# Linear attention with a gated feed-forward: loads held until a transposition has landed

## The chip, the cores and the metric

The kernel runs on one core of a Trainium2 chip. The metric is device time in microseconds (us), the median of several executions. A core has five engines with instruction streams of their own: TensorE (PE in the profile), VectorE (DVE), ScalarE (ACT), GpSimd (POOL) and SyncE (SP). They meet at semaphores. SP and POOL issue most of the DMA transfers, each on a queue of its own, and all queues share the core's 16 DMA engines. An engine executes its instructions in order, so an instruction that waits holds up everything behind it on the same engine.

## The reference

There are 8 batches, 8 heads, 576 positions and 64 dimensions per head. The attention is linear, with phi(x) = elu(x) + 1; then a gated feed-forward network:

```python
def phi(x):
    return np.where(x > 0, x, np.exp(x) - 1.0) + 1.0
q_p, k_p = (phi(q), phi(k))
kv = np.einsum('bhsd,bhse->bhde', k_p, v)
z = np.sum(k_p, axis=2)
num = np.einsum('bhsd,bhde->bhse', q_p, kv)
den = np.einsum('bhsd,bhd->bhs', q_p, z)[..., None] + 1e-06
x = (num / den)                    # to 4608 tokens x 512
a = x @ w1                         # 512 x 1024
b = x @ w2                         # 512 x 1024
h = a * b @ w3                     # 1024 x 1024
out = h @ w_out                    # 1024 x 512
```

## The kernel before

At the start w3 and w_out are multiplied into one 1024 x 512 matrix, so that the feed-forward of a chunk is two products with w1 and w2, an elementwise product, and one more matrix product. A chunk is 512 tokens of one batch; each batch also has a tail of 64 positions, and the tails of all eight batches make up a ninth chunk.

The whole kernel is a list of steps in one string, ORDER, which the last loop walks through. Nothing is rescheduled: the list gives the order of instructions on every engine. A step is a letter, a batch (or chunk) number and a part; a "+" moves it to another engine (for loads from SP to POOL, for copies from ACT to DVE). The letters that matter here:

- L, M, N: load half of a batch's k, q or v, 512 KB each (L95, on SP unless "+"). All three take their buffers from one pool of 13.
- R: load a batch's tail, part 0 for q and k (four transfers of 64 KB), part 1 for v (two) (L104). All R steps around the change are on POOL.
- x and X: the exponential of k and of q on ScalarE (L168). y and Y: max(x, 0) + 1 on DVE (L173). z and Z: the minimum of both, on DVE (L198; L193 for tails), which is phi in bf16. Part 2 is the tail. v: v converted into the tile that also carries a column of ones (L204, L210).
- T: the phi of q transposed by a DMA transposition, on SP (L249). It reads what Z.0, Z.1 and z.2 of that batch wrote.
- K: the kv product of a batch on TensorE (L225, L229) and its copy out of PSUM (L234).
- A: numerator and denominator of 128 positions (L280 on TensorE, reads T's tile), and then 1e-6, reciprocal and product on DVE (L284 to L286). K and A share one PSUM buffer, tagged "at".
- D: the result transposed for the feed-forward, by a DMA transposition on SP (L311). F: eight matmuls with w1 and w2 (L322), the copy of one result by ScalarE (a_sb, L327) and the product by DVE (L328); PSUM has room for two such F at a time. O: the last product (L479) and its copy into an output buffer (L481), two buffers in all. S: the store of an output buffer, 512 KB, on SP (L489).

The steps on SP around the change are, before: T2.0 L3.0 N3.1 L3.1 L4.0 N3.0 S0.1 T3.0 D2.0 S0.0 L4.1 N4.1 M4.0 M4.1 M6.1 D3.0 S1.0 M5.0 N4.0 M5.1 L5.0 T4.0 N5.1 S1.1 M6.0 L5.1 N5.0 N6.0 S2.1 N6.1 T5.0 D4.0 S2.0. On POOL: R4.1 R4.0 R6.0 R6.1 R7.0 R7.1. On PE: K3 O1.3 A3.0 O1.2 A3.2 F2.6 A3.3 F2.3 F2.1 and later F2.5 A3.4 O2.3 F3.7 A2.4; then K4, K5, O3.1, A5.2.

GATES is a second string: "X<Y" gives step X's load a dependency on the transfer of step Y, through `after`. In the kernel before it is empty.

Of the kernel before, what the change touches and what calls it, by code (L numbers as in the profile page):

```python
# [20 lines left out]
def kernel(  # L21
# [77 lines left out]
    def load_tail(b, part, alt):  # L99
        names = ("qk", "v")[part]  # L100
        t = raw[names + "r", b] = ldr.tile([P, len(names), RW], F32, tag="ldr" + names, name=names + "32r")
        for i, name in enumerate(names):
            for g in range(2):
                ins = (nc.gpsimd if alt else nc.sync).dma_start(  # L104
                    out=t[g * R:(g + 1) * R, i].rearrange("p (h d) -> p h d", d=D),
                    in_=src[name][b, g * 4:(g + 1) * 4, NJ * P:S, :].rearrange("h p d -> p h d"))
        return ins

# [137 lines left out]
    def qt_load(b, part):  # L246
        t, s = qt_tile(b), ph["qt", b]
        i = NB if part else 0
        nc.sync.dma_start(out=t[:, i:NB + 2], in_=s[:, i * P:(NB + 2) * P], transpose=True)  # L249

# [412 lines left out]
```

## Time and profile before

| | us |
|---|---|
| median of 3 runs (257.8 to 259.88) | 257.89 |
| the profiled execution's own time | 259.98 |
| its span, from the first to the last instruction | 256.4 |
| PE busy | 231.0 |
| DVE busy | 159.1 |
| ACT busy | 117.1 |
| POOL busy | 48.8 |

The granted clock of TensorE was 0.998 of full speed. All times in the prediction are from the start of the span. In a row of a timeline the first number is the start, the second the duration; then come engine, line, operation, what is written and read, and the count of instructions in the row; the bracket at the end holds the idle time of the engine before the row and what ended it. A row of SP is the time in which SP issued the transfer, not the transfer itself; the views by tile and of the DMA queues give the time from issue to landing.

### The profile page before, as it was taken

Reading aid. Unit: us, or ns where it says so; the run is one execution under the profiler, and the core shown is the slowest. Engines: PE = TensorE matmul, PEld = TensorE weight load, DVE = VectorE, ACT = ScalarE, POOL = GpSimd, SP = SyncE. Lnnn points to the kernel's source line nnn. Section 1 sums busy time; section 2 is a strip of 40 time slices with the busy share of each in tenths; the row PEclk is TensorE's granted clock in tenths of the full one; section 3 lists DMA queues with packets and bytes.
Section 4 is the critical chain, followed back from the end, with each engine's and each line's share of the span. In section 5 each row is a group of like instructions: output and inputs, shape, how many; then the busy total and the mean of one; then the engine's idle time right before and its main releaser. Section 6 shows DMA issues by size and latency. Waiting matters only on the chain.

```text
span 256.4 us, 3789 instructions
## 1 busy us (share of the span) xinstructions
PE 231.0 (90%) x1352; PEld 117.0 (46%) x1368; DVE 159.1 (62%) x350; ACT 117.1 (46%) x180; POOL 48.8 (19%) x84
## 2 busy tenths in 40 slices
PE   0087999999999859999999999999999999999994
PEld 0063665554454424445445445444544444444442
DVE  0548589777998525997887899987244642432300
ACT  2404677247756605756553383544423223233231
POOL 8634479364044300410000000000000000000000
PEclk9999999999999999999999999999999999999999
DMA  6999999999999999799999989736710343000144
GB/s 221 211 238 286 306 261 247 204 229 285 307 239 293 220 213 324 187 289 257 310 355 206 292 246 261 196 63 150 230 20 32 134 83 164 0 3 0 41 143 144
DMA packets 63890, 50.57 MB, mean 197 GB/s; under 512 B 33536, under 2 KB 58368, under 8 KB 63872
## 3 DMA queue, kind: packets, MB, share of 16 engines
q1 hardware_dynamic: 54576, 37.10, 57.2%
q0 software_dynamic: 9152, 13.11, 22.9%
q8 instruction: 10, 0.16, 0.3%
q10 hardware_dynamic: 144, 0.13, 0.1%
q14 instruction: 8, 0.07, 0.1%
HBM read 38.80 MB, written 9.44 MB: 188 GB/s over the span
## 4 chain that ended last, share of the span: by engine, by line
PE 68%; DMA 20%; DVE 4%; issue 3%; SPq 1%; POOL 1%; ACT 1%; DVEq 0%; ACTq 0%; POOLq 0%
PE b_ps L322 22%; PE a_ps L322 22%; PE o_ps L479 18%; DMA w3b<-in_moe_w_dram 9%; DMA out_dram<-o_sb 7%; DMA qk32r<-in_k_dram 3%; PE nd L280 3%; PE kvp L225 2%; SPq L311 1%; DVE y L173 1%; PE o_ps L504 1%; DVE vt L204 1%; ACT a_sb L327 1%; PE kvp L229 1%; DVE kj L198 1%
## 5 line engine op out<-in xcount | busy, mean ns | idle before, releaser
L322 PEld LDWEIGHTS <-w_sb 128*128 128x128 bf16 x576 | 55.1, 98 | 62.8 <-issue 1.6
L328 DVE TENSOR_TENSOR ab<-a_sb,b_ps 128x512 bf16<-128x512 f32 x72 | 49.0, 685 | 39.2 <-PE b_ps L322 28.5
L322 PE MATMUL a_ps<-xt,w_sb 128*128 128x512 bf16 x256 | 66.7, 379 | 0.7 <-ACT a_sb L327 0.6
L322 PE MATMUL b_ps<-xt,w_sb 128*128 128x512 bf16 x256 | 66.7, 379 | 0.2 <-ACT a_sb L327 0.2
L327 ACT COPY a_sb<-a_ps 128x512 f32<-128x512 f32 x72 | 41.8, 586 | 53.1 <-PE a_ps L322 48.7
L479 PE MATMUL o_ps<-wf_sb,ab 128*128 128x512 bf16 x267 | 62.7, 379 | 0.8 <-issue 0.2
L479 PEld LDWEIGHTS <-ab 128*128 128x128 bf16 x280 | 26.9, 98 | 29.9
L481 ACT COPY o_sb<-o_ps 128x512 f32<-128x512 f32 x29 | 16.8, 586 | 43.8 <-PE o_ps L479 33.4
L286 DVE TENSOR_TENSOR xn<-nd,r 128x512 bf16<-128x512 f32 x32 | 22.1, 691 | 1.1
L168 ACT ACTIVATE e<-q 128x1024 bf16<-128x1024 f32 x16 | 16.7, 1055 | 9.4 <-DMA q<-in_q_dram 9.4
L168 ACT ACTIVATE e<-k 128x1024 bf16<-128x1024 f32 x16 | 16.6, 1055 | 4.8 <-DMA k<-in_k_dram 4.8
L280 PE MATMUL nd<-kv,qt 128*128 128x130 bf16 (+1 forms) x160 | 15.8, 220 | 3.1 <-DMA qt<-qj 2.6
L280 PEld LDWEIGHTS <-qt 128*128 128x128 bf16 (+1 forms) x160 | 11.3, 99 | 14.4 <-DMA qt<-qj 3.1
L136 PE MATMUL w3p<-ident,w3b 128*128 128x128 bf16 x64 | 5.7, 242 | 13.2 <-DMA w3b<-in_moe_w_dram 13.2
L284 DVE TENSOR_SCALAR r<-nd 128x8 f32<-128x8 f32 (+1 forms) x40 | 6.4, 161 | 16.2 <-PE nd L280 15.8
L173 DVE TENSOR_SCALAR y<-q 128x1024 bf16<-128x1024 f32 x16 | 11.0, 693 | 7.9 <-DMA q<-in_q_dram 7.9
L143 PE MATMUL wf_ps<-wt_sb,w3t 128*128 128x512 bf16 x61 | 14.8, 379 | 0.8 <-DMA wt_sb<-in_moe_w_out_dram 0.7
L104 POOL DMA_DIRECT2D qk32r<-in_q_dram x14 | 9.0, 648 | 19.2 <-ACT a_sb L327 17.9
L225 PE MATMUL kvp<-vt,kj 128*128 128x130 bf16 x128 | 9.8, 219 | 2.8 <-DVE vt L204 2.0
L198 DVE TENSOR_TENSOR qj<-e,y 128x512 bf16<-128x512 bf16 x32 | 11.9, 416 | 0.4 <-ACT e L168 0.3
L204 ACT CAST vt<-v 128x1024 bf16<-128x1024 f32 x8 | 8.4, 1050 | 7.9 <-DMA v<-in_v_dram 7.9
L198 DVE TENSOR_TENSOR kj<-e,y 128x512 bf16<-128x512 bf16 x32 | 11.9, 418 | 0.2
(54 smaller groups left out, 176.4 us busy)
## 6 DMA issues: line engine op xcount, KB each, us to landing
out_dram<-o_sb SPq DMA_DIRECT2D x15, 512.0 KB, 3.5
q<-in_q_dram SPq DMA_DIRECT2D x13, 512.0 KB, 8.5
k<-in_k_dram SPq DMA_DIRECT2D x13, 512.0 KB, 6.5
v<-in_v_dram SPq DMA_DIRECT2D x12, 512.0 KB, 8.1
w3b<-in_moe_w_dram POOLq DMA_DIRECT2D x8, 256.0 KB, 12.1
...
```

What stands on the lines that cost most here:

```text
L143: nc.tensor.matmul(wfs[i], w3ts[i][:, kc, :], wo_sb[:, kc, :], start=(kc == 0), stop=(kc == FC - 1))
L168: nc.scalar.activation(out=e, in_=x, func=AF.Exp)
L173: (nc.gpsimd if alt else nc.vector).tensor_scalar(out=y, in0=x, scalar1=0.0, scalar2=1.0, op0=ALU.max, op1=ALU.add)
L198: nc.vector.tensor_tensor(out=p[0][:, 2 * g + c].rearrange("p j u d -> p u j d"), in0=e[:, c], in1=y[:, c], op=ALU.min)
L225: nc.tensor.matmul(kvp[:, i, g * W:(g + 1) * W], kj[:, hp, j].rearrange("p u d -> p (u d)"), vt[:, j, 2 * hp:2 * hp + 2, :].rearrange("p h ...
L280: nc.tensor.matmul(nd[rows, g, i * 2 * E1:(i + 1) * 2 * E1], w, kvs[b % 2][:, i, g].rearrange("p u e -> p (u e)"), start=True, stop=True)
L286: nc.vector.tensor_tensor(out=dst.rearrange("p (g h) e -> p g h e", g=2), in0=v4[:, :, :, 0:D], in1=r[rows].unsqueeze(3).to_broadcast([n, ...
L322: nc.tensor.matmul(ps, w[:, kc, f * P:(f + 1) * P], xt_of(c)[:, :, kc, :], start=(kc == 0), stop=(kc == KC - 1))
L327: nc.scalar.copy(out=a_sb, in_=a_ps)
L328: nc.vector.tensor_mul(out=abs_[c][:, f, :], in0=a_sb, in1=b_ps)
L479: nc.tensor.matmul(o_ps, ab[:, f, m * P:(m + 1) * P], wf_sb[:, f, :], start=(f == 0), stop=(f == FC - 1))
L481: copy_of(alt)(out=rows_of(c, m // 2)[:, m % 2], in_=o_ps)
```

## The change

Three things change. First, `load_tail` returns its first transfer instead of its last, `qt_load` returns its transposition, and T steps are remembered, so that GATES can name them: "R4.1<T3.0 R6.0<T4.0" makes POOL's load of batch 4's v tail wait for batch 3's transposition, and the load of batch 6's q and k tail for batch 4's. Second, on SP four loads move: L4.0 from ahead of N3.0 to behind S0.0, and M5.1, L5.0 and M6.1 to behind T4.0. Third, some phi steps move: v4.2, y4.2, x4.2 and z4.2 now stand together between F2.5 and Z4.0; Y5.1 stands behind K4; x6.2 and y6.2 stand behind L6.0. The set of steps is the same.

```diff
     def load_tail(b, part, alt):
         ...
+        first = None
         for i, name in enumerate(names):
             for g in range(2):
                 ins = (nc.gpsimd if alt else nc.sync).dma_start(
                     ...
-        return ins
+                first = first or ins
+        return first
     ...
     def qt_load(b, part):
         ...
-        nc.sync.dma_start(out=t[:, i:NB + 2], in_=s[:, i * P:(NB + 2) * P], transpose=True)
+        return nc.sync.dma_start(out=t[:, i:NB + 2], in_=s[:, i * P:(NB + 2) * P], transpose=True)
     ...
-    Y3.0 y5.2 z3.2 K2 F1.4 A2.2 X3.0 F1.3 L4.0 A2.3 x3.0 O0.1 Z3.0 A2.0 x3.1 N3.0 y3.0 O0.0 v3.1
-    S0.1 A2.1 y3.1 R5.1+ z3.0 z3.1 v3.0 v3.2 O1.1+ O1.0 T3.0 D2.0 S0.0 K3 R4.1+ R4.0+ O1.3 A3.0 O1.2
-    A3.2 L4.1 v4.2+ F2.6 A3.3 F2.3 N4.1 y4.1 F2.1 M4.0 x4.1 A3.1 x4.0 F2.0 M4.1 y4.2 M6.1 v5.2+ x4.2
-    F2.7 Y4.0 D3.0 F2.4 z4.1 X4.1 F2.2 Y4.1 v4.1 S1.0 F2.5 Z4.1 M5.0 N4.0 X4.0 Z4.0 A3.4 z4.2 y4.0
-    O2.3 F3.7 M5.1 Y5.0 v4.0 A2.4 F3.6 z4.0 L5.0 T4.0 R6.0+ x5.2 Y5.1 X5.0 F3.1 N5.1 Z5.0 S1.1 O2.2+
-    K4 F3.2 M6.0 x6.2 X5.1 A4.2 Z5.1 F3.4 z5.2 F3.5 y5.0 A4.1 F3.0 L5.1 F3.3 N5.0 y5.1 X6.1 y6.2
-    O2.1 A4.3 R6.1+ N6.0 S2.1 x5.1 N6.1 v5.0+ T5.0 O2.0 x5.0 v5.1+ A4.0 R7.0+ z5.1 D4.0 z5.0 X6.0
-    O3.3 y7.2 O3.2+ K5+ S2.0 L6.0 z6.2 O3.1 A5.2 L6.1 O3.0 A5.1 D1.1 Y6.1 Z6.1 F4.2 A5.0 Y6.0 F4.5
+    Y3.0 y5.2 z3.2 K2 F1.4 A2.2 X3.0 F1.3 A2.3 x3.0 O0.1 Z3.0 A2.0 x3.1 N3.0 y3.0 O0.0 v3.1 S0.1
+    A2.1 y3.1 R5.1+ z3.0 z3.1 v3.0 v3.2 O1.1+ O1.0 T3.0 D2.0 S0.0 L4.0 K3 R4.1+ R4.0+ O1.3 A3.0 O1.2
+    A3.2 L4.1 F2.6 A3.3 F2.3 N4.1 y4.1 F2.1 M4.0 x4.1 A3.1 x4.0 F2.0 M4.1 v5.2+ F2.7 Y4.0 D3.0 F2.4
+    z4.1 X4.1 F2.2 Y4.1 v4.1 S1.0 F2.5 Z4.1 v4.2+ M5.0 N4.0 X4.0 y4.2 x4.2 z4.2 Z4.0 A3.4 y4.0 O2.3
+    F3.7 Y5.0 v4.0 A2.4 F3.6 z4.0 T4.0 M5.1 L5.0 M6.1 R6.0+ x5.2 X5.0 F3.1 N5.1 Z5.0 S1.1 O2.2+ K4
+    Y5.1 F3.2 M6.0 X5.1 A4.2 Z5.1 F3.4 z5.2 F3.5 y5.0 A4.1 F3.0 L5.1 F3.3 N5.0 y5.1 X6.1 O2.1 A4.3
+    R6.1+ N6.0 S2.1 x5.1 N6.1 v5.0+ T5.0 O2.0 x5.0 v5.1+ A4.0 R7.0+ z5.1 D4.0 z5.0 X6.0 O3.3 y7.2
+    O3.2+ K5+ S2.0 L6.0 x6.2 y6.2 z6.2 O3.1 A5.2 L6.1 O3.0 A5.1 D1.1 Y6.1 Z6.1 F4.2 A5.0 Y6.0 F4.5
     ...
-    GATES = ""
+    GATES = "R4.1<T3.0 R6.0<T4.0"
     ...
         elif t == "T":
-            qt_load(b, i)
+            held[s] = qt_load(b, i)
```

## The prediction

> **What bounds the kernel now.** I read the page's head first, then the idle time in front of TensorE's instructions, then the chain that ended last, then the DMA queues behind it.
>
> ```profile
> span 256.4 us, 3789 instructions
> PE 231.0 (90%) x1352; PEld 117.0 (46%) x1368; DVE 159.1 (62%) x350; ACT 117.1 (46%) x180; POOL 48.8 (19%) x84
> ```
>
> TensorE is busy for 231.0 of 256.4 us, so the change can only win back idle time of PE, or add to it. In the timeline of PE from 59 us to the end only five rows carry idle time in front of them, and these three hold 4.01 us of it (the others have 0.23 and 0.16):
>
> ```profile
> 87.03 0.61 PE L225 MATMUL kvp<-vt,kj 128*128 128x130 bf16 x8 [0.80 <-ACT vt L204]
> ...
> 92.94 0.40 PE L280 MATMUL nd<-kv,qt 128*128 128x130 bf16 x4 [2.62 <-DMA qt<-qj]
> ...
> 99.79 1.02 PE L322 MATMUL a_ps<-xt,w_sb 128*128 128x512 bf16 x4 [0.59 <-ACT a_sb L327]
> ```
>
> In the written order these are K3 (batch 3's kv product), A3.0 (the first natural-layout product of batch 3, which reads the q that T3.0 transposes) and F2.1. After 111 us PE never waits again. The chain of work says what the third hangs on, and the timeline of SP says when things were issued:
>
> ```profile
> 75.05 12.37 DMA out_dram<-o_sb
> ...
> 88.21 3.46 SPq L311
> ...
> 91.77 6.31 DMA out_dram<-o_sb
> ...
> 99.25 0.50 ACT a_sb L327
> ```
>
> ```profile
> 73.30 1.00 SPq L95 DMA_DIRECT2D k<-in_k_dram  x2
> 74.39 0.57 SPq L95 DMA_DIRECT2D v<-in_v_dram  x1
> 75.05 1.98 SPq L489 DMA_DIRECT2D out_dram<-o_sb  x1
> 81.09 6.24 SPq L249 DMA_TRANSPOSE qt<-qj  x1
> 87.42 4.25 SPq L311 DMA_TRANSPOSE xt<-xn  x1
> ```
>
> The store S0.1 (75.05) lands at 87.42, and T3.0, ready at 81.09, holds SP until just then: a transposition's issue ends when what is ahead of it on the queue has drained. T3.0 itself lands at 92.9, where A3.0's wait ends. D2.0 and the store S0.0 queue behind it; S0.0 lands at 98.08 and frees the output buffer that ScalarE's copy for O1.3 needs, and behind that copy stand the a_sb copies that F2.1 waits for. So one backlog of transfers at 75 to 81 us costs all of the 4 us.
>
> The second limit is the DMA engines. In the table of windows, columns after DVE, ACT and POOL are the clock, the DMA share and GB/s:
>
> ```profile
> 124.00:134.00 10.00, 9.95 (x54) 4.79 (x54) 8.45 (x19) 5.01 (x8) 0.00 (x0) 1.00 1.10 372
> 88.00:92.00 4.00, 2.28 (x17) 1.11 (x15) 0.20 (x1) 1.07 (x3) 1.23 (x2) 1.00 1.56 101
> ```
>
> Saturated with 512 KB loads they move 372 GB/s, or 1.41 us for one load; with T3.0, D2.0 and tails together, 101.
>
> **The change, part by part.**
>
> *T3.0 freed of company.* Ahead of it or beside it went L4.0 (the second k of the row at 73.30, 512 KB) and, from POOL, these tails of batches 4 and 6:
>
> ```profile
> 74.25 1.23 POOL L104 DMA_DIRECT2D v32r<-in_v_dram  x2 [11.50 <-DVE vr L210]
> 75.47 1.29 POOL L104 DMA_DIRECT2D qk32r<-in_q_dram  x2
> 76.75 1.23 POOL L104 DMA_DIRECT2D qk32r<-in_k_dram  x2
> 77.97 1.23 POOL L104 DMA_DIRECT2D qk32r<-in_q_dram  x2
> 80.91 0.62 POOL L104 DMA_DIRECT2D qk32r<-in_k_dram  x1 [1.71 <-DMA v32r<-in_v_dram]
> ```
>
> Nine tails of 64 KB are 0.59 MB, 1.6 us at 372 GB/s; with L4.0 it is 3.0 us less. S0.1 then lands between 84.4 and (nothing saved) 87.4; I take 84.4. How long after the drain a transposition lands:
>
> ```profile
> 114.41 5.78 SPq L249 DMA_TRANSPOSE qt<-qj  x1
> ...
> DMA to landing us min/median/max: 7.8/7.8/7.8
> ```
>
> T4.0's issue ended at 120.19 and it landed at 114.41 + 7.8 = 122.2, 2.0 later; T3.0 needed 92.9 - 87.4 = 5.5, with tails beside it. So T3.0 lands between 86.4 and 89.9; I take 88, since no tail runs beside it now. The v load at 74.39, for which K3 waited 0.80, also comes sooner, so A3.0 is due at 92.94 - 2.62 - 0.80 = 89.5, after 88: both waits go. Every us by which T3.0 is later than 89.5 comes back in full. S0.0 landed 5.1 after T3.0; it now lands near 93.1, and up to 1.1 later because batch 4's six tails (0.39 MB, 1.1 us) enter right then. F2.1, due at 99.79 - 4.01 = 95.8, needs S0.0 plus the 1.7 us from 98.08 to 99.79, 94.8 to 95.9. Gain at F2.1: 4.0, between 1.5 (S0.0 2.5 late) and 4.0.
>
> *L4.0 behind S0.0.* It comes about 1.4 us ahead of L4.1, N4.1, M4.0 and M4.1 in the queue, but M6.1 leaves that group, so the five loads there are still five. I cost it at nothing: the exponentials of k wait behind F2.1's copy anyway.
>
> *POOL.* Its waiting instruction R4.1 has R4.0 behind it, R6.0 has R6.1, R7.0 and R7.1; POOL does nothing else after 42 us, so the waits hold up only tails. R4 is issued from 88 to 92 (six pieces at 0.65) and first read when DVE is past Z4.1, near 108. R7.0 is first read by y7.2:
>
> ```profile
> 137.01 0.42 DVE L173 TENSOR_SCALAR yr<-qk32r 128x512 bf16<-128x512 f32 x1
> ```
>
> Less the gain that is 134. R7.0 is the seventh to tenth of twelve pieces issued from T4.0's landing on (near 115, below), so issued by about 122: 12 us of cover for its landing. Without it DVE, and K5's copy behind y7.2, would be late by what is missing.
>
> *The phi steps of batch 4's tail.* Here DVE has new work at a tight place. In the timeline of DVE, the mul of F2.5, then Z4.1 and Z4.0 together, then the three operations of A3.4 (from 112.76), then z4.2:
>
> ```profile
> 110.70 0.69 DVE L328 TENSOR_TENSOR ab<-a_sb,b_ps 128x512 bf16<-128x512 f32 x1 [0.44 <-PE b_ps L322]
> 111.31 1.42 DVE L198 TENSOR_TENSOR qj<-e,y 128x512 bf16<-128x512 bf16 x4
> 112.76 0.17 DVE L284 TENSOR_SCALAR r<-nd 64x8 f32<-64x8 f32 x1
> ...
> 113.19 0.69 DVE L286 TENSOR_TENSOR xnr<-nd,r 64x512 bf16<-64x512 f32 x1
> 113.92 0.43 DVE L193 TENSOR_TENSOR qj<-er,yr 128x512 bf16<-128x512 bf16 x1
> ```
>
> ```profile
> 114.43 0.41 PE L280 MATMUL nd<-kv,qt 128*64 128x130 bf16 x4
> ```
>
> That PE row is A2.4. It writes the single PSUM buffer tagged "at" that A3.4's L286 reads until 113.88. The new order puts v4.2, y4.2 and z4.2 between F2.5's mul and A3.4's operations:
>
> ```profile
> 96.38 0.61 DVE L210 CAST vr<-v32r 64x256 bf16<-64x256 f32 x2
> ...
> 104.84 0.42 DVE L173 TENSOR_SCALAR yr<-qk32r 128x512 bf16<-128x512 f32 x1
> ```
>
> 0.61 + 0.42 + 0.43 = 1.46 us. F2.5's mul is released by PE (its own 0.44 of waiting says so), so nothing taken off DVE earlier helps. L286 ends at 113.88 + 1.46 = 115.34, 0.9 after A2.4 is due: a new wait of 0.9 us, between 0 (DVE elsewhere ahead) and 1.5. The gain from here is 3.1.
>
> *M5.1, L5.0 and M6.1 behind T4.0, twelve tails of 6 and 7 too.* T4.0 itself is now ready when DVE ends Z4.0, at 112.73 + 1.46 - 4.0 = 110.2, with little ahead. The price is at T5.0:
>
> ```profile
> 120.23 0.58 SPq L95 DMA_DIRECT2D v<-in_v_dram  x1
> ...
> 126.93 0.44 SPq L95 DMA_DIRECT2D v<-in_v_dram  x1
> 127.48 7.84 SPq L249 DMA_TRANSPOSE qt<-qj  x1
> ```
>
> From issue to landing, the load of 120.23 (N5.1) and the transposition of 127.48 (T5.0) took
>
> ```profile
> DMA to landing us min/median/max: 5.0/5.0/5.0
> ```
>
> ```profile
> DMA to landing us min/median/max: 11.7/11.7/11.7
> ```
>
> and A5.2, which reads T5.0's q, starts at
>
> ```profile
> 140.45 0.39 PE L280 MATMUL nd<-kv,qt 128*128 128x130 bf16 x4
> ```
>
> Today N5.1 lands at 125.2, T5.0 at 127.48 + 11.7 = 139.2, and A5.2 reads it at 140.45: only 1.3 us to spare. T5.0's issue ended at 135.3, when N6.1 had landed, seven transfers after N5.1 (1.44 us each); the landing followed 3.9 later. After the change A5.2 is due at 140.45 - 3.1 = 137.4. T4.0's issue, with nothing ahead, takes 2.7 us (T7.0's:)
>
> ```profile
> L249 SPq DMA_TRANSPOSE qt<-qj x1: 2671/2671/2671, 170.0 to 170.0; - x1
> ...
> DMA to landing us min/median/max: 4.5/4.5/4.5
> ```
>
> so M5.1 is issued at 113.0 and lands 5.0 later, at 118.0. Ten more transfers to N6.1 at 1.44 make 132.4; twelve tails, 0.79 MB, 2.1 us at 372 GB/s, make 134.5. T5.0 lands 2.0 (like T4.0) to 3.9 (like itself) later: 136.5 to 138.4. I take 138.4, its own row: a wait of 1.0 at A5.2, between 0 and the 5.7 of the third rival.
>
> The Trainium skill speaks against that price: Advanced Engine Details and Errata, section X-Bar Transpose (TRN2), says that transposing DMAs on this chip are as fast as regular ones. By it T5.0 would cost no more than a load's step, and the sum would be 1.0 better; the drain-to-landing figures above, 2.0 to 5.5 against 1.44, do not agree with it.
>
> *Sum.* 4.0 - 0.9 - 1.0 = 2.1 us. Against the profiled execution's 259.98 us (span 256.4, 3.6 around it) that is 257.9. The median of the runs shown is 2.1 below the profiled one; taking 2.1 off 257.89 gives **255.8**. The median run may lack some of the profiled stalls; that is in the second rival.
>
> **The rivals.**
>
> 1. *T5.0 hides.* If a transposition follows the drain by one load's step, 1.44, T5.0 lands at 135.9, A5.2 waits for nothing, the gain stays 3.1: 254.8; 253.9 if A2.4's wait also fails to appear. For it: T4.0's 2.0. Against: T5.0's 3.9. The rule of the Trainium skill quoted above is this case.
> 2. *It doesn't do what it says.* T3.0 and S0.0 land about as late as before, or the unprofiled runs had little to win there. If 1.5 of the 4.0 is won, and 0.9 lost at A2.4, the time is 257.3. For it: T3.0's 5.5 after the drain at 87.4 was long, and I know only that tails ran beside it; the profiled run is 2.1 above the median. Against: L4.0 and nine tails were plainly ahead of it or beside it.
> 3. *Slower: the tails of 6 and 7 choke the stretch before T5.0.* They enter in twelve pieces at 0.65 us on POOL, 7.8 us, among loads. If the engines then run as at 88 to 92, at 101 instead of 372 GB/s, 7.8 x (1 - 101/372) = 5.7 us are lost, T5.0 lands at 144.1, A5.2 starts 3.7 later than today: 261.5. It decides from 140.45: a T5.0 landing later than that makes the kernel slower. For it: that window. Against: T4.0 has landed when they start, and no transposition runs beside them until T5.0.
>
> **How the numbers follow.** Forecast 0.42 (own range 254.8 to 256.8: T5.0 between 137.4 and 139.4); rival 1 0.15; rival 2 0.25 (256.8 to 258); rival 3 0.18, half of it beyond 260.5. About 1% (2.6 us) is what a measurement can tell from no change. Faster by more than that (under 255.3): a third of the forecast and rival 1, 0.29. Slower by more (over 260.5): 0.13 with what I have not seen. The rest, 0.58, lies within 1%. The range 254.2 to 260.3 leaves out the best end of rival 1 and the worse half of rival 3.
>
> **What would show it.** T3.0 landing by 89.5 and no idle time before A3.0 shows the first step; S0.0 landing by 94 and none before F2.1, the second. A wait of some 0.9 us of nd for L286 near 111 us shows the squeeze on DVE. A wait of nd for qt near 137 us, and T5.0 landing within a us of 138.4, shows the fourth; waits of DVE for R7.0 at y7.2 would be a step that I have missed. The prediction is wrong if T3.0 lands late although alone, or if T5.0 lands after 140.45.

## The result, and the profile after

The changed kernel takes 257.29 us (median of 14 runs, 256.22 to 258.84), the kernel before 258.7 beside it (257.33 to 260.57). The ratio is 0.9955, with a 95% interval of 0.9933 to 0.9977: a gain of 0.45%, 1.2 us, where 2.1 were forecast. A ratio here is computed from the single executions, without those more than 1.5% above the fastest of their kernel, so it need not equal the ratio of the two medians, which are 1.41 us apart. The gain lies within the 1% that was called no change, inside the range, and is a little over half of what was worked out. The time itself, 257.29, is 1.5 above the forecast 255.8; 0.8 of that is the kernel before, which takes 258.7 over more runs and not 257.89. The span of the profiled execution went from 256.4 to 255.5. The page's head for the kernel after:

```profile
span 255.5 us, 3806 instructions
...
PE 233.0 (91%) x1368; PEld 117.4 (46%) x1368; DVE 159.4 (62%) x350; ACT 117.5 (46%) x180; POOL 48.2 (19%) x84
```

PE's busy time is 2.0 us longer with 1368 records in the trace against 1352, for the same matmuls; it says nothing on the work. So positions are compared, not busy times. These are the rows of PE's timeline from 59 us on that have idle time in front of them, in the kernel after; lines above 109 are two higher than before, L282 is L280 and L324 is L322:

```profile
70.93 1.02 PE L324 MATMUL b_ps<-xt,w_sb 128*128 128x512 bf16 x4 [0.32 <-ACT a_sb L329]
...
110.50 0.41 PE L282 MATMUL nd<-kv,qt 128*64 128x130 bf16 x4 [0.96 <-DVE xnr L288]
...
130.67 0.40 PE L282 MATMUL nd<-kv,qt 128*128 128x130 bf16 x4 [0.57 <-DVE xn L288]
...
138.51 0.40 PE L282 MATMUL nd<-kv,qt 128*128 128x130 bf16 x4 [1.01 <-DMA qt<-qj]
...
141.19 1.02 PE L324 MATMUL a_ps<-xt,w_sb 128*128 128x512 bf16 x4 [0.33 <-DMA xt<-xn]
...
152.03 1.02 PE L324 MATMUL b_ps<-xt,w_sb 128*128 128x512 bf16 x4 [0.28 <-ACT a_sb L329]
```

The first row stands ahead of what the change reaches. The others are A2.4, A4.0, A5.2, F4.2 and F4.1. The waits at K3, A3.0 and F2.1 are gone, as forecast; five smaller ones stand behind them. The two steps that waited longest before now start here, with no idle time ahead:

```profile
89.02 0.39 PE L282 MATMUL nd<-kv,qt 128*128 128x130 bf16 x4
...
94.88 1.03 PE L324 MATMUL a_ps<-xt,w_sb 128*128 128x512 bf16 x4
```

A3.0 at 89.02 and F2.1 at 94.88 are 3.92 and 4.91 us earlier than before. From there the lead is given back. The start of each step on PE, read from the two timelines, and how far the kernel after is ahead:

| step | before | after | ahead | lost since the row above, to |
|---|---|---|---|---|
| F2.5 | 108.70 | 103.74 | 4.96 | |
| A2.4 | 114.43 | 110.50 | 3.93 | 1.03, DVE's xnr (the squeeze) |
| A4.2 | 122.87 | 118.89 | 3.98 | |
| A4.0 | 133.91 | 130.67 | 3.25 | 0.73, DVE's xn |
| A5.2 | 140.45 | 138.51 | 1.94 | 1.31, T5.0's q |
| F4.2 | 142.63 | 141.19 | 1.44 | 0.50, D4.0's x |
| F4.4 | 153.89 | 152.89 | 1.01 | 0.43, ScalarE's a_sb |
| F5.7 | 157.80 | 156.93 | 0.87 | 0.14 |
| F7.0, the last F | 238.74 | 237.88 | 0.86 | 0.01 |

The column adds up: 4.96 - 1.03 - 0.73 - 1.31 - 0.50 - 0.43 - 0.14, and 0.04 of rounding and small shifts back, is 0.86; the spans differ by 0.88.

The transfers behind it, in SP's timeline of the kernel after. In order: T3.0, D2.0, S0.0, T4.0, N6.1, T5.0, D4.0.

```profile
81.20 2.67 SPq L251 DMA_TRANSPOSE qt<-qj  x1
84.07 3.16 SPq L313 DMA_TRANSPOSE xt<-xn  x1
87.32 0.53 SPq L491 DMA_DIRECT2D out_dram<-o_sb  x1
...
109.34 2.67 SPq L251 DMA_TRANSPOSE qt<-qj  x1
...
124.09 0.68 SPq L95 DMA_DIRECT2D v<-in_v_dram  x1
124.89 11.41 SPq L251 DMA_TRANSPOSE qt<-qj  x1
136.83 1.97 SPq L313 DMA_TRANSPOSE xt<-xn  x1
```

The views by line give the times from issue to landing; these are T3.0's, S0.0's, T4.0's, N6.1's, T5.0's and D4.0's:

```profile
DMA to landing us min/median/max: 6.4/6.4/6.4
...
DMA to landing us min/median/max: 4.4/4.4/4.4
...
DMA to landing us min/median/max: 4.6/4.6/4.6
...
DMA to landing us min/median/max: 12.2/12.2/12.2
...
DMA to landing us min/median/max: 13.6/13.6/13.6
...
DMA to landing us min/median/max: 4.3/4.3/4.3
```

T3.0 now lands at 87.6 (before 92.9), S0.0 at 91.7 (98.08), T4.0 at 113.9 (122.2). But T5.0 lands at 138.46 against 139.19, and D4.0 at 141.15 against 140.93: PE had five us of lead, and these two transfers are hardly earlier or not at all. That is the question for the experiments.

One row of DVE's timeline explains A4.0. It is y5.1, which stands ahead of A4.3's operations and waits for L5.1's k:

```profile
128.88 0.69 DVE L175 TENSOR_SCALAR y<-k 128x1024 bf16<-128x1024 f32 x1 [1.67 <-DMA k<-in_k_dram]
```

### The profile page after: what moved, and what is told of

The parts are those of the page before. It is cut to its first block, busy times and chain, and to the rows that moved or that the text cites. A ratio compares the mean times of both kernels' runs of the same rounds, so it can differ in the third digit from the quotient of the medians.

```text
span 255.5 us, 3806 instructions
## 1 busy us (share of the span) xinstructions
PE 233.0 (91%) x1368; PEld 117.4 (46%) x1368; DVE 159.4 (62%) x350; ACT 117.5 (46%) x180; POOL 48.2 (19%) x84
## 4 chain that ended last, share of the span: by engine, by line
PE 57%; DMA 28%; DVE 4%; issue 3%; POOL 3%; SPq 2%; ACT 1%; DVEq 0%; ACTq 0%; POOLq 0%
PE o_ps L481 18%; PE b_ps L324 17%; PE a_ps L324 17%; DMA k<-in_k_dram 7%; DMA v<-in_v_dram 5%; DMA out_dram<-o_sb 5%; DMA w_sb<-in_moe_w_dram 4%; DMA wt_sb<-in_moe_w_out_dram 3%; DMA qk32r<-in_q_dram 2%; PE nd L282 2%; PE kvp L227 2%; POOL w_sb L116 2%; SPq L313 1%; ACT a_sb L329 1%; PE o_ps L506 1%
## 5 line engine op out<-in xcount | busy, mean ns | idle before, releaser
L324 PEld LDWEIGHTS <-w_sb 128*128 128x128 bf16 x576 | 55.1, 98 | 63.0 <-issue 1.6
L324 PE MATMUL b_ps<-xt,w_sb 128*128 128x512 bf16 x256 | 66.7, 379 | 0.6 <-ACT a_sb L329 0.6
L324 PE MATMUL a_ps<-xt,w_sb 128*128 128x512 bf16 x256 | 66.7, 379 | 0.3 <-DMA xt<-xn 0.3
L481 PE MATMUL o_ps<-wf_sb,ab 128*128 128x512 bf16 x280 | 64.4, 379 | 0.0
L282 PE MATMUL nd<-kv,qt 128*128 128x130 bf16 (+1 forms) x160 | 15.8, 220 | 3.0 <-DMA qt<-qj 1.0
L282 PEld LDWEIGHTS <-qt 128*128 128x128 bf16 (+1 forms) x160 | 11.3, 99 | 14.5 <-DVE xn L288 3.0
L145 PE MATMUL wf_ps<-wt_sb,w3t 128*128 128x512 bf16 x64 | 16.0, 395 | 0.6 <-DMA wt_sb<-in_moe_w_out_dram 0.5
L175 DVE TENSOR_SCALAR y<-k 128x1024 bf16<-128x1024 f32 x16 | 11.0, 687 | 3.1 <-DMA k<-in_k_dram 3.0
L105 POOL DMA_DIRECT2D v32r<-in_v_dram x12 | 7.5, 630 | 26.4 <-DMA qt<-qj 25.3
```

Of the source, the lines that this page charges most:

```text
L105: ins = (nc.gpsimd if alt else nc.sync).dma_start(out=t[g * R:(g + 1) * R, i].rearrange("p (h d) -> p h d", d=D), in_=src[name][b, g * 4:( ...
L145: nc.tensor.matmul(wfs[i], w3ts[i][:, kc, :], wo_sb[:, kc, :], start=(kc == 0), stop=(kc == FC - 1))
L175: (nc.gpsimd if alt else nc.vector).tensor_scalar(out=y, in0=x, scalar1=0.0, scalar2=1.0, op0=ALU.max, op1=ALU.add)
L282: nc.tensor.matmul(nd[rows, g, i * 2 * E1:(i + 1) * 2 * E1], w, kvs[b % 2][:, i, g].rearrange("p u e -> p (u e)"), start=True, stop=True)
L324: nc.tensor.matmul(ps, w[:, kc, f * P:(f + 1) * P], xt_of(c)[:, :, kc, :], start=(kc == 0), stop=(kc == KC - 1))
L481: nc.tensor.matmul(o_ps, ab[:, f, m * P:(m + 1) * P], wf_sb[:, f, :], start=(f == 0), stop=(f == FC - 1))
```

## The experiments

The kernels were timed against the kernel before; a ratio is to that one. Diffs are of the tokens of ORDER and of GATES, against the changed kernel where nothing else is said. "Ahead" is PE's lead over the kernel before in the profiled executions, as in the table above.

### Each hold alone

Only the first hold: M5.1, L5.0 and M6.1 at their old places, the tails of 6 and 7 free to start when POOL gets to them.

```diff
-GATES = "R4.1<T3.0 R6.0<T4.0"
+GATES = "R4.1<T3.0"
-... F2.0 M4.1 v5.2+ ...  O2.3 F3.7 Y5.0 v4.0 A2.4 F3.6 z4.0 T4.0 M5.1 L5.0 M6.1 R6.0+ x5.2 X5.0 ...
+... F2.0 M4.1 M6.1 v5.2+ ...  O2.3 F3.7 M5.1 Y5.0 v4.0 A2.4 F3.6 z4.0 L5.0 T4.0 R6.0+ x5.2 Y5.1 X5.0 ...
     (and x6.2, y6.2 back to their old places)
```

> The first hold alone: R4 behind T3.0, L4.0 behind S0.0, batch 4's tail phi steps as in the change; M5.1, L5.0, M6.1 and the tails of 6 and 7 go where they went before, ahead of T4.0. Theory A (the second hold gives the gain back, because it pushes three loads and twelve tails, 2.2 + 4.2 us of transfer, into the stretch between T4.0 and T5.0): PE still stands 4.9 us earlier than before at F2.1, T4.0 lands near 117 and costs nothing, T5.0 lands near 134 and A5.2 waits for nothing; the gain kept is 3.5 to 4, about 255. Theory B (the engines are full from 81 to 139 us, so T5.0 lands near 138.5 in whatever order the same bytes go ahead of it): A5.2 waits 1 us as in the changed kernel, time within 0.5 of the changed kernel's 257.3.

259.92 us, ratio 1.0032 (0.9997 to 1.0066). F2.1 is 5.30 ahead, yet A4.2 is 1.04 behind. PE's idle rows:

```profile
107.19 0.82 PE L481 MATMUL o_ps<-wf_sb,ab 128*128 128x512 bf16 x3 [1.06 <-DVE ab L330]
...
112.63 0.41 PE L282 MATMUL nd<-kv,qt 128*64 128x130 bf16 x4 [1.42 <-DVE xnr L288]
...
123.91 0.40 PE L282 MATMUL nd<-kv,qt 128*128 128x130 bf16 x4 [2.73 <-DMA qt<-qj]
```

The last row is the reader of T4.0. The tails of 7, M5.1 and L5.0 are on their way beside T4.0, which is issued at 111.47 and lands at 123.86, where the kernel before had 122.22 and the changed one 113.91. So the lead won at T3.0 is lost one transposition later. Neither theory of the expectation saw this wait. That the second hold is what costs the changed kernel its gain falls with this: without it there is no gain.

Only the second hold: the kernel before, with M5.1, L5.0 and M6.1 behind T4.0, the gate R6.0<T4.0, and Y5.1, x6.2 and y6.2 moved with them. Against the kernel before (the three function changes that GATES needs are in):

```diff
-GATES = ""
+GATES = "R6.0<T4.0"
-... M4.1 y4.2 M6.1 v5.2+ ...  O2.3 F3.7 M5.1 Y5.0 ...  z4.0 L5.0 T4.0 R6.0+ x5.2 Y5.1 X5.0 ...
+... M4.1 y4.2 v5.2+ ...  O2.3 F3.7 Y5.0 ...  z4.0 T4.0 M5.1 L5.0 M6.1 R6.0+ x5.2 X5.0 ...
```

> The second hold alone: M5.1, L5.0, M6.1 behind T4.0 and the tails of 6 and 7 behind T4.0; L4.0, R4 and batch 4's tail phi steps as before. T3.0 has only R6's four tails less beside it (0.26 MB, 0.7 us), so A3.0 still waits about 2 us. Theory A: what is won there is small and T5.0 comes later than before (139.2) by the transfers pushed behind T4.0, less T4.0's own earlier landing: 140 to 143, a wait of 0 to 2 us at A5.2, time 0 to 2 us slower than before. Theory B: T5.0 again near 139, no wait at A5.2, 0.5 to 1 us faster than before.

259.38 us, ratio 1.0032 (1.0008 to 1.0056). T3.0 lands at 90.38, since the tails of 6 are out of its way by this gate too, and F2.1 is 2.98 ahead; but T5.0 lands at 140.56, 1.37 later than before, A5.2 waits 1.35 and is 0.16 behind; this is what theory A expected, not B. Each half alone is slower or no better, both together are faster. As these traces read, a hold pays only as long as the reader of the next transposition isn't reached by what was held.

### The gate on batch 4's tail

The changed kernel with only the gate of T4.0, so that R4 may run beside T3.0:

```diff
-GATES = "R4.1<T3.0 R6.0<T4.0"
+GATES = "R6.0<T4.0"
```

> The changed kernel with R4 free to load as early as before; only R6 and R7 are held. Six tails, 1.1 us at 372 GB/s or 1.9 at 0.31 each, are back ahead of T3.0. By the prediction T3.0 lands 1.1 to 2 us later, at 88.7 to 89.6, on the edge of A3.0's 89.0, so PE waits 0 to 0.6 there, and F2.1 has the rest of the gain. R4 is then out of the way of the loads after S0.0. Capacity theory: since T5.0 is still behind the same bytes it lands near 138.5 and the time is that of the changed kernel within 0.5.

258.25 us, ratio 0.9978 (0.9948 to 1.0009). T3.0 lands at 89.42 instead of 87.60, F2.1 is 4.41 ahead instead of 4.91, and the end 0.15 instead of 0.86. Not all of this is the gate's: in this profiled execution PE was already 0.45 behind at F1.5, ahead of what the change reaches, and T3.0 was issued 0.49 later. From issue to landing T3.0 takes 7.73 instead of 6.40, so six tails of 64 KB ahead of it or beside it cost it 1.3 us, 0.22 each, and PE read it without a wait all the same. The interval overlaps the changed kernel's: that the gate on batch 4's tail is worth anything is not shown.

### The phi steps of batch 4's tail

v4.2, y4.2 and z4.2 behind A3.4 take the squeeze on DVE away:

```diff
-F2.5 Z4.1 v4.2+ M5.0 N4.0 X4.0 y4.2 x4.2 z4.2 Z4.0 A3.4 y4.0
+F2.5 Z4.1 M5.0 N4.0 X4.0 x4.2 Z4.0 A3.4 v4.2+ y4.2 z4.2 y4.0
```

> The changed kernel, but v4.2, y4.2 and z4.2 behind A3.4's operations on DVE instead of ahead of them. Both theories: the wait of 0.96 us at A2.4 goes, and T4.0, which needs z4.2, is issued about 1 us later. A and B alike say that T5.0 then lands at the same time or up to 1 us later, so PE waits up to 1 us more at A5.2 and the time stays within 0.5 of the changed kernel's. If A2.4's wait were a loss of its own, the time would be 1.0 lower.

258.52 us, ratio 1.0012 (0.9981 to 1.0043). A2.4's wait is gone (5.03 ahead there), and nothing came of it. z4.2 is what T4.0 waits for, so T4.0 is issued 1.2 later and all loads behind it are too; L5.1 lands at 129.97, and y5.1 of DVE waits for it:

```profile
130.00 0.69 DVE L175 TENSOR_SCALAR y<-k 128x1024 bf16<-128x1024 f32 x1 [3.89 <-DMA k<-in_k_dram]
```

A4.0 then waits 2.80 us, and PE is 0.75 ahead at A5.2. About 1.4 us of the loss up to there has no wait in front of it: behind A4.0 the granted clock of TensorE falls to 0.53 from 131 to 134 us and 0.85 from 134 to 136, which is 1.7 us of its work. Eight of the twelve executions have a mean clock of 0.993 or less; the other four take 257.97 to 260.21, no less than the changed kernel. And T5.0 landed at 138.90, so that A5.2 could not have been more than 1.55 ahead. The 0.96 us at A2.4 were not won here: later waits take the same time back.

### Less in front of T5.0

The changed kernel once more, as a measure of how far one kernel differs from itself:

> The changed kernel once more, for comparison on the same chip: 0.993 to 0.998 of the kernel before. Slack theory (formed from the runs so far: the transfers from T5.0 on land when the bytes ahead of them are through, almost whatever the order, so what PE has won at a place cannot be more than the slack that the transfer read there had before, plus what it lands earlier): A5.2 stands 1.3 + (139.2 - T5.0's landing) us earlier than before, F4.2 1.7 + (140.9 - D4.0's landing).

257.39 us, ratio 0.9942 (0.992 to 0.9964), the same as the first time. In this profiled execution T5.0 landed at 137.59, A5.2 was 2.81 ahead and the end 1.78, so profiled executions of one kernel differ by 0.9. The loss behind A5.2 is the same in both: 1.08 and 1.03.

Two loads, M5.1 and L5.0, ahead of T4.0 again:

```diff
-... M5.0 N4.0 X4.0 ... F3.6 z4.0 T4.0 M5.1 L5.0 M6.1 R6.0+
+... M5.0 N4.0 M5.1 X4.0 ... F3.6 z4.0 L5.0 T4.0 M6.1 R6.0+
```

> The changed kernel with M5.1 and L5.0 ahead of T4.0 again; M6.1 and the tails of 6 and 7 stay behind it. In the changed kernel N4.0 has landed at 110.7 and the engines move 155 GB/s from 110 to 114, while T4.0 goes alone and SP holds nothing else. Capacity theory (T5.0 lands when the bytes ahead of it are through, so only an idle stretch of the engines that is filled brings it forward): the two loads land by 113.6, T4.0 by 115.6 to 116, ahead of A4.2 at 118.9, no wait there, and T5.0 lands 1.5 to 2.5 us earlier than 138.5, near 136.5; A5.2 waits for nothing; 1 to 2 us faster than the changed kernel. If T4.0's early landing is what makes the change faster, this is slower than the changed kernel.

256.95 us, ratio 0.9919 (0.9889 to 0.995). T5.0 was expected at 136.5, as the two loads were to fill an idle stretch of the DMA engines, and landed at 138.64, though two loads less stood between T4.0 and it. The transfers ahead of T5.0 are the same bytes, in another order. The same kernel again:

> M5.1 and L5.0 ahead of T4.0, once more beside the changed kernel. By the slack theory the two differ by no more than T5.0's and D4.0's landings do, 0.2 us or less one way or the other, since the 2.9 us of loads only changed places with T4.0; if the 0.36% between their two medians so far is real, it shows again.

257.48 us, ratio 0.9968 (0.9938 to 0.9997), T5.0 at 138.46. The two intervals together can't be told from the changed kernel's.

With the phi move of above added to it, and y5.1 behind A4.3 so that A4.0 can't wait for it:

```diff
-F2.5 Z4.1 v4.2+ M5.0 N4.0 M5.1 X4.0 y4.2 x4.2 z4.2 Z4.0 A3.4 y4.0 ... N5.0 y5.1 X6.1 O2.1 A4.3
+F2.5 Z4.1 M5.0 N4.0 M5.1 X4.0 x4.2 Z4.0 A3.4 v4.2+ y4.2 z4.2 y4.0 ... N5.0 X6.1 O2.1 A4.3 y5.1
```

> M5.1 and L5.0 ahead of T4.0, v4.2, y4.2 and z4.2 behind A3.4, and y5.1 behind A4.3. The wait of 1 us at A2.4 goes; T4.0, issued 1.2 us later but still draining behind L5.0, lands near 116; DVE no longer stands at y5.1 for L5.1 with A4.3 behind it. Capacity theory: PE reaches A5.2 one us earlier, at 135.5, and waits there for T5.0 at 136.5, so the time is at most 0.5 better than with M5.1 and L5.0 ahead alone. If the engines' waits for DVE were losses of their own, 1 to 1.5 us better.

258.34 us, ratio 0.9975 (0.9938 to 1.0012). PE has no wait up to A4.0 and is 5.19 ahead there; then K5 waits 1.98 for DVE's kj and A5.2 1.10 for T5.0, which lands at 138.81. It ends 0.65 ahead. Two waits in front of T5.0 were removed, and T5.0's landing took back all of it.

So no reordering of these loads brought T5.0 ahead of where the changed kernel's two profiled executions have it. What is left are the bytes ahead of it. The tails of 6 and 7 behind T5.0, twelve transfers of 64 KB less:

```diff
-GATES = "R4.1<T3.0 R6.0<T4.0"
+GATES = "R4.1<T3.0 R6.0<T5.0"
-T4.0 M5.1 L5.0 M6.1 R6.0+ x5.2 ... A4.3 R6.1+ N6.0 S2.1 x5.1 N6.1 v5.0+ T5.0 O2.0 ... S2.0 L6.0 x6.2 y6.2 z6.2 O3.1
+T4.0 M5.1 L5.0 M6.1 x5.2 ... A4.3 N6.0 S2.1 x5.1 N6.1 v5.0+ T5.0 R6.0+ R6.1+ O2.0 ... S2.0 L6.0 O3.1
     (x6.2, y6.2, z6.2 behind F4.7, y7.2 behind x7.2)
```

> The changed kernel, but the twelve tails of batches 6 and 7 wait for T5.0 instead of T4.0 (their phi steps behind F4.7 and x7.2). Takes 0.79 MB, 2.1 us of transfer, out of the way of T5.0. A and B alike: T5.0 lands near 136.4, A5.2 (due at 137.4 without its wait, 136.8 if L5.1 no longer holds up DVE) waits for nothing, L5.1 lands before 128 and A4.0's 0.57 goes: 1.5 to 2 us faster than the changed kernel, 255.5. If it is not the tails but T5.0's own slowness after the drain that sets it, no change.

261.3 us, ratio 1.0104 (1.0066 to 1.0142): the slowest of all, although T5.0 lands at 134.82 and A5.2 is 3.77 ahead. The view of T5.0's line, and then PE's and ScalarE's idle rows behind it:

```profile
DMA to landing us min/median/max: 10.9/10.9/10.9
```

```profile
149.55 0.41 PE L282 MATMUL nd<-kv,qt 128*64 128x130 bf16 x4 [1.40 <-DVE xn L288]
...
151.29 1.87 PE L324 MATMUL a_ps<-xt,w_sb 128*128 128x512 bf16 x4 [1.32 <-ACT a_sb L329]
...
159.29 1.04 PE L324 MATMUL a_ps<-xt,w_sb 128*128 128x512 bf16 x4 [0.63 <-DMA xt<-xn]
```

```profile
145.55 0.63 ACT L170 ACTIVATE er<-qk32r 128x512 bf16<-128x512 f32 x1 [1.36 <-DMA qk32r<-in_k_dram]
...
149.71 1.06 ACT L170 ACTIVATE e<-k 128x1024 bf16<-128x1024 f32 x1 [1.63 <-DMA k<-in_k_dram]
```

ScalarE stands still for the tail of batch 6 (x6.2) and for L7.0 (x7.0), with the a_sb copies of batch 4's F behind it, and D5.0, behind the same bytes, lands late for F5.7. Twelve tails were worth 138.46 - 134.82 = 3.6 us at T5.0 (2.8 against the second profile of the changed kernel), and more than that was lost a batch later: PE goes from 3.77 ahead at A5.2 to 1.49 behind at F5.7. But the three waits hold only 3.35 of these 5.26 us. The row at 151.29 shows what else is lost: its four matmuls take 1.87 us where others take 1.02. The windows there, in which the third number from the end is the granted clock:

```profile
150.00:152.00 2.00, 0.71 (x2) 0.25 (x2) 0.89 (x3) 1.95 (x5) 0.00 (x0) 0.78 1.32 172
152.00:154.00 2.00, 2.00 (x6) 0.76 (x5) 1.88 (x5) 1.17 (x2) 0.00 (x0) 0.50 1.10 265
154.00:156.00 2.00, 2.00 (x10) 0.84 (x8) 1.58 (x4) 0.34 (x1) 0.00 (x0) 0.87 1.22 102
```

The clock is short by 2 x (0.22 + 0.50 + 0.13) = 1.7 us of work. All seven executions of this kernel have a mean clock of 0.986 to 0.993, and 1.7 of 258 us is 0.7%, so those near 0.987 lost about twice that; in the profiles of the kernel before and of the changed one the clock stays at 1.00 here. How much of the 1.0104 is the waits and how much the clock, no run tells apart.

Only the tails of 7 behind T5.0, on top of the two loads ahead of T4.0:

```diff
-GATES = "R4.1<T3.0 R6.0<T4.0"
+GATES = "R4.1<T3.0 R6.0<T4.0 R7.0<T5.0"
-v5.0+ T5.0 O2.0 x5.0 v5.1+ A4.0 R7.0+ z5.1 ... O3.3 y7.2 O3.2+ ... F5.7 x7.2
+v5.0+ T5.0 R7.0+ O2.0 x5.0 v5.1+ A4.0 z5.1 ... O3.3 O3.2+ ... F5.7 x7.2 y7.2
```

> The kernel with M5.1 and L5.0 ahead of T4.0, and besides the six tails of batch 7 behind T5.0 (y7.2 behind x7.2). Six tails at the 0.31 us that twelve of them cost when they were moved (T5.0 at 134.8 against 138.5) bring T5.0 another 1.9 us forward, to 134.6. Capacity theory: they land among L6, L7 and D5.0 instead, and D5.0 and the a_sb copies behind x7.0 come later by as much, so the time is no better than with M5.1 and L5.0 ahead alone, 0 to 1 us worse. If T5.0 alone were the bound, 1 us better.

258.49 us, ratio 0.9992 (0.9957 to 1.0028). The same picture with half of the tails: T5.0 at 137.20, A5.2 3.21 ahead; then PE waits 1.77 for a product of batch 4's F, as DVE and ScalarE wait for L6.1 and L7.0, and at F4.4 PE is 1.76 behind. Again 1.7 us of this are a clock of 0.50 around 153 us; only three of the twelve executions have such a mean clock (0.992 or less), and the profiled one, 259.92 us, is one of them.

### Where the lead goes behind A5.2

What is left to tell apart is whether the lead goes to the bytes, so that something has to be late, or to readers that stand too early on in-order engines. First the loads: with R7 behind T5.0, SP issues D5.0 ahead of batch 7's loads, and x7.0 stands behind F5.7. Against the last kernel:

```diff
-x6.1 L7.0 x6.0 M7.0 A5.3 D3.1 x7.0 z6.1 F4.0 ... S3.0 F4.4 D5.0 A5.4 ... F5.7 x7.2 y7.2 ... T6.0
+x6.1 x6.0 A5.3 D3.1 z6.1 F4.0 ... F4.4 D5.0 L7.0 M7.0 M7.1 L7.1 T6.0 S3.1 S3.0 N7.0 A5.4 ... F5.7 x7.0 x7.2 y7.2
```

> M5.1 and L5.0 ahead of T4.0, batch 7's tails behind T5.0, and on SP D5.0 ahead of the loads L7.0, M7.0 and of the stores S3.0, S3.1, T6.0 ahead of both stores and of N7.0; x7.0 behind F5.7, so that ScalarE no longer stands at it with a_sb copies behind. Slack theory: T5.0 lands near 137.2, A5.2 stands 3.2 earlier than before, and since D5.0 and T6.0 now have less ahead of them, the gain is kept to the end: 2.5 to 3.2 us faster than before, about 0.989. If what follows A5.2 is lost to something other than the transfers ahead of D5.0 and T6.0 and the wait at x7.0, the gain falls back to 1 us or less after 145 us, as it did without this reordering (1.8 us slower than before at F5.7).

256.85 us, ratio 0.9932 (0.9905 to 0.996): 3.66 ahead at A5.2, 2.46 at F4.2 (D4.0), 1.54 at F4.4, 1.41 at the end. Then all twelve tails behind T5.0:

```diff
-GATES = "R4.1<T3.0 R6.0<T4.0 R7.0<T5.0"
+GATES = "R4.1<T3.0 R6.0<T5.0"
-T4.0 M6.1 R6.0+ x5.2 ... A4.3 R6.1+ N6.0 ... T5.0 R7.0+ O2.0 ... L6.0 x6.2 y6.2 z6.2 O3.1 ... z6.1 F4.0
+T4.0 M6.1 x5.2 ... A4.3 N6.0 ... T5.0 R6.0+ R6.1+ R7.0+ O2.0 ... L6.0 O3.1 ... z6.1 F4.0 x6.2 y6.2 z6.2
```

> The same with all twelve tails of 6 and 7 behind T5.0. Slack theory: T5.0 lands near 134.8, which is earlier than PE needs it, so A5.2 stands 4.0 earlier (A2.4's 1.0 stays lost); the tails, 3.7 us, then lie ahead of D5.0 and T6.0, and x6.2 waits for them on ScalarE near 146 us. 2.5 to 4 us faster than before if they get through in time; if not, waits of a_sb and of nd for DVE near 146 to 150 us, and 1 us or less is left.

256.88 us, ratio 0.9929 (0.99 to 0.9958). A5.2 and F4.2 are both 4.19 ahead, with no wait; at F4.4 1.72 are left. The rows of DVE, ScalarE and PE between them:

```profile
146.86 0.69 DVE L175 TENSOR_SCALAR y<-k 128x1024 bf16<-128x1024 f32 x1 [1.47 <-DMA k<-in_k_dram]
```

```profile
146.91 2.00 ACT L170 ACTIVATE e<-k 128x1024 bf16<-128x1024 f32 x2 [2.79 <-DMA k<-in_k_dram]
```

```profile
148.20 1.02 PE L324 MATMUL b_ps<-xt,w_sb 128*128 128x512 bf16 x4 [0.96 <-DVE ab L330]
```

y6.1 on DVE and x6.1 on ScalarE are released together, by L6.1, and both have the copies and products of batch 4's F behind them. If that is the whole loss, moving those two readers back (x6.0 and z6.1 with them) wins it, with every transfer as it is:

```diff
-Y6.0 F4.5 y6.1 F4.7 v6.0+ x6.1 x6.0 A5.3 D3.1 z6.1 F4.0 x6.2 y6.2 z6.2 v6.1+ v6.2 F4.6 A4.4
+Y6.0 F4.5 F4.7 v6.0+ A5.3 D3.1 F4.0 y6.1 x6.1 x6.2 y6.2 z6.2 v6.1+ v6.2 F4.6 x6.0 z6.1 A4.4
```

> All twelve tails behind T5.0 and D5.0 ahead of the loads, as in the run before, and the phi steps of batch 6's k two F later: y6.1 and x6.1 behind F4.0, x6.0 and z6.1 behind F4.6. Where they stood, DVE waited 1.47 and ScalarE 2.79 us for L6.1 with F's work behind them. Slack theory: those waits go, A5.3, F4.4 and with them D5.0 come up to 2 us earlier, and 2 to 3.5 us against the kernel before are left at the end, 0.987 to 0.992. If the bytes bound whatever the place of their readers, the waits turn up at x6.2 or at D5.0 and the ratio stays at 0.993.

255.41 us, ratio 0.9877 (0.9836 to 0.9917): 1.2% under the kernel before, and faster than the changed one (0.9933 to 0.9977). Only six executions were timed; the profiled one, 254.56, is 0.85 under their median. Its page's head, and all rows of PE's timeline from 59 us to the end that have idle time ahead of them:

```profile
span 252.5 us, 3790 instructions
...
PE 230.4 (91%) x1352; PEld 117.0 (46%) x1368; DVE 159.0 (63%) x350; ACT 117.1 (46%) x180; POOL 48.6 (19%) x84
```

```profile
105.81 1.67 PE L481 MATMUL o_ps<-wf_sb,ab 128*128 128x512 bf16 x7 [0.16 <-issue]
...
110.17 0.41 PE L282 MATMUL nd<-kv,qt 128*64 128x130 bf16 x4 [0.96 <-DVE xnr L288]
```

PE is 4.3 ahead from A2.4 to F4.3 without a loss, and 3.90 at the end. L6.1 lands at 144.74, after y6.1's old place and before its new one. The same move of the readers in the kernel with R7 behind T5.0 and D5.0 ahead of batch 7's loads:

```diff
-Y6.0 F4.5 y6.1 F4.7 v6.0+ x6.1 x6.0 A5.3 D3.1 z6.1 F4.0 v6.1+ v6.2 F4.6 A4.4
+Y6.0 F4.5 F4.7 v6.0+ A5.3 D3.1 F4.0 y6.1 x6.1 v6.1+ v6.2 F4.6 x6.0 z6.1 A4.4
```

> Batch 7's tails alone behind T5.0, D5.0 ahead of the loads, and batch 6's k phi two F later. F4.2 keeps its wait of 1 us for D4.0, which lands at 140.1; from there the 2.5 us won are kept instead of falling to 1.4: 0.990 to 0.991. If the bytes bound, 0.993 as without the move.

255.97 us, ratio 0.9899 (0.9867 to 0.9931), from 0.9932 (0.9905 to 0.996), with intervals that overlap: 2.40 ahead at the end, from 1.41. And the same move in the changed kernel, no load touched (x7.0 behind F4.4 as well):

```diff
-Y6.0 F4.5 y6.1 F4.7 v6.0+ x6.1 L7.0 x6.0 M7.0 A5.3 D3.1 x7.0 z6.1 F4.0 v6.1+ v6.2 F4.6 A4.4 ... S3.0 F4.4 D5.0
+Y6.0 F4.5 F4.7 v6.0+ L7.0 M7.0 A5.3 D3.1 F4.0 y6.1 x6.1 v6.1+ v6.2 F4.6 x6.0 z6.1 A4.4 ... S3.0 F4.4 x7.0 D5.0
```

> The changed kernel with batch 6's k phi two F later and x7.0 behind F4.4; no load moves. Slack theory: the 0.28 us wait of b_ps for a_sb near 152 us and the 0.4 us that the changed kernel loses between F4.2 and F4.4 go; A5.2 and F4.2 still stand behind T5.0 and D4.0. 0.2 to 0.5 us faster than the changed kernel, 0.993 or so; D5.0 behind the same loads may take it back at F5.7.

257.31 us, ratio 0.9954 (0.993 to 0.9978): nothing. The 0.43 at F4.4 is gone in its trace, but there T5.0 and D4.0 are what is late, and no reader's place changes that. Neither edit alone was told apart from the changed kernel: the bytes had to go from ahead of T5.0 and D4.0, and the readers of what then came later had to stand later. Last, the phi steps of batch 4's tail behind A3.4 in the best kernel:

```diff
-F2.5 Z4.1 v4.2+ M5.0 N4.0 M5.1 X4.0 y4.2 x4.2 z4.2 Z4.0 A3.4 y4.0
+F2.5 Z4.1 M5.0 N4.0 M5.1 X4.0 x4.2 Z4.0 A3.4 v4.2+ y4.2 z4.2 y4.0
```

> As the first of this set, and besides v4.2, y4.2 and z4.2 behind A3.4 on DVE, which takes away the wait of 1 us at A2.4. Where T5.0 bounded, that gained nothing (1.0012 against 0.9955). Here T5.0 lands near 134.5 and A5.2 would be due at 135.3: PE gains the 1.0 us at A2.4 and keeps it to A5.2 and F4.2, where D4.0 (137.1) is due at 137.4. By the slack theory it is lost later unless D5.0 follows; 0 to 1 us better than the first of this set.

255.73 us, ratio 0.9873 (0.9842 to 0.9904), not to be told from 0.9877. Once more the move wins no time that can be measured. (T5.0 was expected near 134.5 and landed at 136.20 in the profiled execution, which is 2.0 above the median.)

## Why the prediction was right or wrong

**T3.0 freed of company: the waits go as forecast, the landing is right in part by luck.** T3.0 was put at 88, it landed at 87.60. But its two terms are off. S0.1, the store ahead of it, in the changed kernel:

```profile
74.58 0.77 SPq L491 DMA_DIRECT2D out_dram<-o_sb  x1
```

```profile
DMA to landing us min/median/max: 8.0/8.0/8.0
```

It landed at 82.55, not 84.4: without L4.0 and nine tails it needed 8.0 us where it had needed 12.4, which is 4.4 less and not the 3.0 that bytes at 372 GB/s gave. T3.0 then landed 5.05 after it and not 3.6, although no tail was on its way (POOL issues R4 from 88.17 on). The two misses cancel to 0.4, and the reason given for T3.0's 5.5 before, the tails beside it, is not borne out; why T3.0 takes 6.40 from issue to landing where T4.0 takes 4.57 stays open. S0.0 was put at 93.1 and landed at 91.7, 4.1 behind T3.0 instead of 5.2. K3's, A3.0's and F2.1's waits are gone, the one on S0.0's buffer with them. F2.1's gain was 4.91, above the range of 1.5 to 4.0 that the step gave: the three brackets that went hold 4.01, and the rest lies in shorter gaps and in what a bracket leaves out (F2.1 follows the matmuls before it 0.76 sooner, its bracket had 0.59). Rival 2, that the change doesn't do what it says, is refuted by these rows, although its time, 257.3, is the one that came out (beside a kernel before at 258.7, not 257.89). Its other half, that unprofiled runs had little to win, falls too: 123 other executions of the kernel before have a median span of 256.5 us, the profiled one 256.4, so its extra 2.1 us lay outside the span.

**L4.0 behind S0.0, and POOL's waits: right.** No row of PE waits for either, and no row of DVE waits for R7.

**The squeeze on DVE: right.** 0.9 forecast, 0.96 in the row of A2.4. What the step didn't see is that the 0.9 isn't to be had: with it taken away, T4.0 is later.

**The second hold: the right number from two wrong terms.** T5.0 was put at 138.4 and landed at 138.46; a wait of 1.0 was forecast at A5.2, the row has 1.01. But the twelve tails were priced at 2.1 us, 0.18 each, from a stretch of 512 KB loads. Taken away they brought T5.0 forward by 3.6 us, 0.30 each; the six tails of 7, in the kernel with two loads ahead of T4.0, were worth 1.4 us (138.64 to 137.20), and in the two later kernels with that hold 2.65 (135.99 in both). And N6.1's landing to T5.0's was priced at 3.9, from the kernel before; it was 138.46 - 136.25 = 2.2. N6.1 itself, put at 134.5, landed at 136.25, 1.75 later. The two misses cancel, and that is luck. Rival 3's mechanism, that the tails choke that stretch, is there, but at 1.5 us beyond the 2.1 where it had 5.7, about a quarter; T5.0 stays under 140.45, and so it doesn't decide.

**The sum: this is the step that failed.** "4.0 - 0.9 - 1.0 = 2.1" ends at A5.2, and there it was right: 1.94 ahead. It carries no term for A4.0 (0.73, y5.1 waiting for L5.1, hidden in the total by the 0.9 too little at F2.1) and puts what comes behind A5.2 at nothing without a reason, and there 1.08 of the 1.94 went: 0.50 to D4.0, 0.43 to a_sb, 0.14 at F5.7. D4.0 could have been read from the kernel before. These rows are D4.0's issue, its time to landing, and F4.2, the first matmul that reads it:

```profile
135.87 3.13 SPq L311 DMA_TRANSPOSE xt<-xn  x1
```

```profile
DMA to landing us min/median/max: 5.1/5.1/5.1
```

```profile
142.63 0.38 PE L322 MATMUL a_ps<-xt,w_sb 128*128 128x512 bf16 x1
```

It landed at 140.93 and was read at 142.63, a slack of 1.70 us. If D4.0 lands when it lands today, F4.2 can gain 1.70 and no more, whatever was won before it. A5.2 had 140.45 - 139.19 = 1.26. So a reader's gain is at most its slack before plus how much earlier its transfer lands. This is arithmetic, since no reader starts before its transfer has landed. What the traces add is that the bound was met within 0.05 us wherever PE waited at A5.2; T5.0's landing, then A5.2's gain in us by this rule and as read (the three kernels left out agree as closely):

| kernel | T5.0 lands | by the rule | read |
|---|---|---|---|
| the second hold alone | 140.56 | -0.11 | -0.16 |
| without the R4 gate | 139.47 | 0.98 | 0.93 |
| two loads ahead of T4.0 | 138.64 | 1.81 | 1.76 |
| the changed kernel | 138.46 | 1.99 | 1.94 |
| the changed kernel again | 137.59 | 2.86 | 2.81 |
| two ahead, R7 behind T5.0 | 137.20 | 3.25 | 3.21 |

And all kernels that have the same bytes ahead of T5.0 land it between 137.6 and 140.6, in whatever order and however early T4.0 is. The windows from T3.0's issue to A5.2, first of the kernel before, then of the changed one, show how full the DMA engines are:

```profile
81.00:138.00 57.00, 52.54 (x301) 25.74 (x302) 40.80 (x97) 31.82 (x49) 6.51 (x10) 1.00 1.10 260
```

```profile
81.00:138.00 57.00, 54.97 (x322) 27.31 (x320) 43.14 (x100) 32.33 (x49) 11.16 (x18) 1.00 1.04 260
```

They move 260 GB/s in both, with the DMA engines' mean share (the number before it) above 1: the change reorders a stream that is nearly full. It isn't full everywhere. These are the 3 us around T4.0's issue in the changed kernel and in the one with two loads ahead of T4.0:

```profile
108.00:111.00 3.00, 2.04 (x13) 0.85 (x11) 2.77 (x8) 1.30 (x3) 0.00 (x0) 1.00 0.54 168
```

```profile
108.00:111.00 3.00, 2.04 (x13) 0.86 (x12) 2.84 (x8) 0.59 (x1) 0.00 (x0) 1.00 1.05 359
```

The second fills the gap, and T5.0 is no earlier for it: from 114 to 117 us it moves 193 GB/s where the changed kernel moves 342. So it is shown that the order of these transfers moves T5.0 by little, within 137.6 to 140.6; that the engines' capacity alone is the reason is not shown. What the change won at T3.0 it could keep only as far as the next readers had slack.

**Rival 1, T5.0 hides: refuted by its landing,** though not by its reason. It was built on T5.0 following N6.1 by one load's step, and 2.2 us is nearer to that (1.44) than to the 3.9 that was taken; the tails used up the difference. The rule of the Trainium skill beside it (Advanced Engine Details and Errata, X-Bar Transpose (TRN2): transposing DMAs are as fast as regular ones) therefore did better than the prediction allowed, though T5.0's 2.2 is still more than a load's step.

**What stays open.** Why F5.7's and F4.4's last 0.57 us were lost in the changed kernel can be read as D5.0 and ScalarE's wait for L7.0, and the trace with x7.0 moved lost nothing at F4.4; but 0.43 us is below what the times tell apart. The step from 0.9929 to 0.9877 has intervals that overlap (0.99 to 0.9958, 0.9836 to 0.9917); that it is real rests on the idle rows that went. What sets TensorE's clock to half in the traces with long waits is open: the kernel before waits 2.62 us at A3.0 and keeps a clock of 1.00 from 88 to 96 us.
